# Where finished products leave PSUM, which engine does the differences, and the queue of the w_out jobs

## The chip, the cores and the metric

The kernel runs on one core of one Trainium2 chip. Its engines are TensorE (PE in the rows, PEld for its weight loads), VectorE (DVE), ScalarE (ACT), GpSimd (POOL) and SyncE (SP, here a queue that issues DMAs). Each works through its own instructions in order and waits for the others by semaphores. The metric is the device time of one execution in microseconds, the median of the runs of a kernel.

## The reference

A windowed attention over 4 x 576 tokens with 8 heads of 64, then two MLPs of width 512 and inner width 2048 over the 2304 tokens, all in float32:

```python
def reference(**kwargs):
    attn_out = _attn_ref(**attn_kwargs)
    x = attn_out.transpose(0, 2, 1, 3).reshape(B * S, H * D)
    x = _moe_ref(x=x, **moe_kwargs)
    return _moe2_ref(x=x, **moe2_kwargs)

def _moe_ref(x, w_in, w_out, s, b):
    h = x @ w_in
    r = np.maximum(h, 0.0)
    return (s * (r * r) + b) @ w_out

def _moe2_ref(x, w_in, w_out):
    h = x @ w_in
    return (h * np.cos(h)) @ w_out
```

## The kernel before

**Precision.** A float32 operand is cut into a high and a low part of TensorE's float32r form; a product is then three matmuls (high by high, high by low, low by high). A cut is a cast on ScalarE (the high part) and a difference on VectorE (the low part).

**First MLP.** 80 steps `p`: five token tiles of 384 or 512 columns (`t`), 16 blocks of the inner width each (`fc`). A step does `mm_in` (12 matmuls), `relu2` on ScalarE and VectorE, and `out_step` of the step two before (`LAG`; 12 matmuls). The attention and the work on the second MLP's weights are hung between the steps by `at(...)` and fired at three phases of a step.

**Jobs.** In the last 16 steps of the first MLP eight jobs prepare w_out of the second. `job_load(i)` fetches two raw blocks from DRAM into a tile `a` of seven slots, `job_sums(i)` fills the other slots (the seven weight combinations of a 2 by 2 product in seven multiplications), `job_split(i)` cuts them and stores both parts to `cut_out` in DRAM. Job 0 is summed in step 67, and the next ones follow at 1.5 steps on average. Tile `a` has two buffers, so the load of job i + 2 waits until the last store from job i's tile has landed. Loads and stores are issued by SP, in order with all its other DMAs.

**Second MLP.** Three token blocks `i` of 768 columns (`NS`), 16 inner blocks each: 48 steps `n`. Step `n` of the loop at the end issues `mm_h(n)`, 24 matmuls of 384 columns into a PSUM pair `h`, of which three are in turn, so that `mm_h(n)` needs `cos_g(n - 3)` to be done. The activation h cos h is a chain: `cos_n(n)` (ScalarE adds MAGIC), `cos_r(n)` (subtracts it again, on ScalarE or VectorE by its flag, then `r` on VectorE), `cos_q(n)` (VectorE), and a step later `cos_s(n - 1)` (two passes on ScalarE) and `cos_g(n - 1)` (VectorE, writes `G`).

The second product is done in seven products M1 to M7 over the 2 by 2 blocks of `G` and w_out. Each is four units `k` of 12 matmuls; `unit_cut(u)` cuts the operand of a unit, and `cut_to` runs it up to two units ahead of TensorE in the loop. Some operands are differences of others (`sub`). Units 0 to 3 run in steps 6, 10, 14 and 18, from step 19 on two in every step but 31 and 33, and the last 26 after the loop. So a product ends with every second step.

For the first two token blocks all products add up in one PSUM tile, `yy`:

```python
    fresh = j in ("M1", "M2", "M7") or (i == NS - 1 and j == "M4")
    ...
    if k == 3:
        evac[:] = [(i, j)]
```

After its last unit a product is in `evac`, and the next call of `evacuate()` copies it out: M1, M5 and M6 by `keep` on ScalarE (`s`, `v`, `r`), M3 by `send` on ScalarE, M2, M7 and M4 by `send` on VectorE (line 675, `o`). The next product's first unit waits for that copy. In the loop the call stands behind the chain of the step and ahead of its units; the units behind it are on TensorE after `mm_h(n)`.

Of the kernel before, what the change touches and what calls it, by code (L numbers as in the profile page):

```python
# [74 lines left out]
def attention_then_two_mlps(ctx, tc, qk_p, qk_d, v_p, v_d, mask_p, mask_d, w1, w2, sv, bv, out):  # L75
# [134 lines left out]
    def job_load(i):  # L210
        a = after_att[0].tile([P, 7, 256], F32, tag=f"job{i % 2}", name=f"job{i}")
        two = lambda fc: whole_out[fc].rearrange("p (e n) -> p e n", e=2)
        nc.sync.dma_start(a[:, 0:6:5, :], two(2 * i))
        nc.sync.dma_start(a[:, 4:7:2, :], two(2 * i + 1))
        jobs[i] = a

    def job_sums(i):
        a = jobs[i]
        for to, x, y, op in ((1, 5, 6, ALU.add), (2, 1, 0, ALU.subtract), (3, 4, 2, ALU.subtract), (5, 0, 5, ALU.subtract)):
            nc.gpsimd.tensor_tensor(out=a[:, to, :], in0=a[:, x, :], in1=a[:, y, :], op=op)  # L220

    def job_split(i):
        a = jobs.pop(i)
        for lo, hi in ((0, 4), (4, 7)):
            h = wpool.tile([P, hi - lo, 256], F32R, tag=f"wh{2 * (i % 2) + lo // 4}", name=f"jh{i}_{lo}")
            nc.scalar.copy(h, a[:, lo:hi, :])
            nc.vector.tensor_tensor(
                out=a[:, lo:hi, :].bitcast(F32R), in0=a[:, lo:hi, :], in1=h.bitcast(F32), op=ALU.subtract
            )
            nc.sync.dma_start(cut_out[:, lo:hi, i, 0, :], h.bitcast(F32))  # L230
        nc.sync.dma_start(cut_out[:, :, i, 1, :], a)
# [274 lines left out]
    def w_in_load(n):  # L506
        if n >= NH:
            return
        place, tag = (wpool, f"wl{n}") if n < 4 else (home[0], f"wi{n % 4}")
        win[n] = place.tile([P, 2, DM], F32R, tag=tag, name=f"wi{n}")  # L510
        nc.sync.dma_start(win[n].bitcast(F32), cut_in[n % NFC])
# [52 lines left out]
    def cos_g(n):  # L564
        i, fc = divmod(n, NFC)
        f, k, z = fc % 2, fc // 4, fc // 2 % 2
        if z == 0:
            G[i, f, k] = home[0].tile([P, 2, 2, SB], F32, tag=f"G{i % 2}{f}{k}", name=f"G{i}_{f}_{k}")
        g = G[i, f, k]
        nc.vector.scalar_tensor_tensor(  # L570
            out=g[:, :, z, :], in0=ns.pop(n), scalar=-1.0, in1=hp.pop(n), op0=ALU.add, op1=ALU.mult
        )
        if f == 0 and z == 1:
            sub(i, g[:, 1], g[:, 1], g[:, 0], nc.gpsimd)
            ops[i, k, "M1"], ops[i, k, "M5"] = g[:, 0], g[:, 1]
        if f == 1 and z == 1:
            ops[i, k, "M2"], ops[i, k, "M3"] = g[:, 0], g[:, 1]

    def sub(i, out, a, b, eng):
        eng.tensor_tensor(out=out, in0=a, in1=b, op=ALU.subtract)  # L580
# [12 lines left out]
    def unit_cut(u):  # L593
# [7 lines left out]
        if j == "M5" and not last:  # L601
            t2 = G[i, 0, k][:, 1]
            sub(i, t2, G[i, 1, k][:, 1], t2, nc.gpsimd)
            ops[i, k, "M6"] = t2
            b11 = G[i, 0, k][:, 0]
            sub(i, b11, t2, b11, nc.gpsimd)
            ops[i, k, "M7"] = b11
        if j == "M2" and last:
            t2 = home[0].tile([P, 2, SB], F32, tag=f"G{1 - i % 2}0{k}", name=f"t2_{k}")
            sub(i, t2, G[i, 1, k][:, 1], G[i, 0, k][:, 1], nc.gpsimd)  # L610
            ops[i, k, "M6"] = t2
            b11 = G[i, 0, k][:, 0]
# [65 lines left out]
    def evacuate():  # L678
# [4 lines left out]
        if i < NS - 1:  # L683
# [35 lines left out]
    with tc.manual_schedule():  # L719
# [216 lines left out]
        for n in range(1, NH):  # L936
# [17 lines left out]
            evacuate()  # L954
# [101 lines left out]
```

## Time and profile before

| what | value |
|---|---|
| median of 2 runs | 1008.63 us (1005.95 to 1011.32) |
| profiled execution, whole | 1007.53 us |
| its span, first to last instruction | 1005.70 us |
| mean granted clock of TensorE | 0.959 of full speed |
| TensorE busy | 910.3 us, 91% |
| VectorE busy | 638.4 us, 63% |
| ScalarE busy | 519.6 us, 52% |
| GpSimd busy | 142.2 us, 14% |

The span is that of the instructions; the execution's own time is 1.83 us longer. Busy time of TensorE is modelled from pipelined matmuls and hides stretches in which it runs at its lower clock, so the timeline in blocks of equal work says more than the share.

### The profile page before, as it was taken

To read this page: it belongs to the slowest core of one execution; us is meant where nothing else is said; L and a number is where in the kernel's file an instruction comes from. 1 tells how busy PE (TensorE), PEld (TensorE's weight loads), DVE (VectorE), ACT (ScalarE), POOL (GpSimd) and SP (SyncE) were. 2 spreads that over 40 slices of the span, in tenths; PEclk is the share of its full clock that TensorE was granted. 3 is DMA by queue.
4 is the path that set the end of the run, shared out by engine and by line. 5 is a ranking of instruction groups with operands and counts; after the bars stand their busy time and mean duration, and the time that the engine had idled before them with its cause. 6 is when DMAs were issued, how large, how long until landed. Compare 5 with 4: busy or idle time off the path is not lost. (4 is left out here: it accounts for less than half of the span.)

```text
span 1005.7 us, 13928 instructions
## 1 busy us (share of the span) xinstructions
PE 910.3 (91%) x5148; PEld 806.6 (80%) x5148; DVE 638.4 (63%) x1001; ACT 519.6 (52%) x1057; POOL 142.2 (14%) x94
## 2 busy tenths in 40 slices
PE   8999999999999999998788788878779888877888
PEld 6666699988888888886678788878779888877888
DVE  6888877665557665774436667655546655544753
ACT  6776777754556555544435655344334434333433
POOL 1000000000000000032220002502200430300740
PEclk9999999999999999999899999998889998999899
DMA  9956143343434554576798335444445454543566
GB/s 265 337 203 211 51 136 117 107 167 96 164 115 162 172 165 141 190 225 231 260 302 347 105 105 168 147 146 135 147 141 182 140 176 129 171 150 100 172 198 211
DMA packets 76050, 173.08 MB, mean 172 GB/s; under 512 B 7024, under 2 KB 35152, under 8 KB 75984
## 3 DMA queue, kind: packets, MB, share of 16 engines
q1 hardware_dynamic: 75840, 172.01, 52.4%
q8 instruction: 41, 0.67, 0.3%
q14 instruction: 25, 0.20, 0.1%
q10 hardware_dynamic: 144, 0.20, 0.1%
HBM read 135.48 MB, written 36.70 MB: 171 GB/s over the span
## 5 line engine op out<-in xcount | busy, mean ns | idle before, releaser
L645 PE MATMUL yy_M<-op,wo 128*128 128x384 f32 x1008 | 204.8, 364 | 59.6 <-DVE o L675 18.0
L645 PEld LDWEIGHTS yy_M<-op,wo 128*128 128x128 f32 x1008 | 196.1, 209 | 66.0 <-issue 29.2
L534 PE MATMUL h<-x,wi 128*128 128x384 f32 x1152 | 212.0, 341 | 19.4 <-issue 13.2
L534 PEld LDWEIGHTS h<-x,wi 128*128 128x128 f32 x1152 | 204.5, 192 | 22.9 <-issue 18.2
L543 ACT ACTIVATE n<-h,pmagic 128x768 f32<-128x768 f32 x48 | 43.1, 900 | 150.5 <-PE h L534 150.5
L599 DVE TENSOR_TENSOR op<-G,op 128x768 fp32r<-128x768 f32 x80 | 93.3, 1185 | 41.0 <-ACT op L598 41.0
L440 PE MATMUL y<-g,wh 128*128 128x512 f32 (+1 forms) x256 | 99.4, 388 | 8.6 <-DVE g L497 8.6
L598 ACT CAST op<-G 128x768 fp32r<-128x768 f32 x80 | 65.0, 830 | 77.1 <-PE yy_M L645 36.8
L425 PE MATMUL h<-xs,wh 128*128 128x512 f32 (+1 forms) x256 | 99.0, 387 | 0.0
L441 PE MATMUL y<-g,wh 128*128 128x512 f32 (+1 forms) x256 | 97.8, 382 | 0.2 <-DVE g L498 0.2
L442 PE MATMUL y<-g,wl 128*128 128x512 f32 (+1 forms) x256 | 97.6, 381 | 0.0
L427 PE MATMUL h<-xs,wl 128*128 128x512 f32 (+1 forms) x256 | 96.4, 377 | 0.0
L426 PE MATMUL h<-xs,wh 128*128 128x512 f32 (+1 forms) x256 | 96.4, 376 | 0.0
L550 DVE TENSOR_SCALAR n<-n 128x768 f32<-128x768 f32 x40 | 25.8, 644 | 109.1 <-ACT n L543 109.1
L220 POOL TENSOR_TENSOR job<-job 128x256 f32<-128x256 f32 x32 | 25.5, 808 | 477.8 <-DVE wa L145 407.9
L330 ACT ACTIVATE sm<-sm,nmax 96x80 f32<-96x80 f32 (+1 forms) x140 | 49.5, 355 | 49.2 <-DVE nmax L327 49.2
L580 POOL TENSOR_TENSOR G<-G 128x768 f32<-128x768 f32 x20 | 45.3, 2265 | 192.9 <-DVE G L570 169.3
L552 DVE SCALAR_TENSOR_TENSOR r<-n,h 128x768 f32<-128x768 f32 x48 | 45.8, 954 | 33.7 <-ACT n L548 26.7
L489 ACT ACTIVATE r<-h 128x512 f32<-128x512 f32 (+1 forms) x80 | 43.9, 548 | 43.2 <-PE h L427 39.4
L440 PEld LDWEIGHTS y<-g,wh 128*128 128x128 f32 x256 | 48.9, 191 | 16.8 <-DVE g L497 9.5
L497 DVE CAST g<-r 128x512 fp32r<-128x512 f32 (+1 forms) x64 | 26.6, 416 | 52.7 <-ACT r L495 47.0
L441 PEld LDWEIGHTS y<-g,wh 128*128 128x128 f32 x256 | 49.0, 191 | 8.4 <-DVE g L498 1.0
(104 smaller groups left out, 1423.0 us busy)
## 6 DMA issues: line engine op xcount, KB each, us to landing
wo<-cut_out SPq DMA_DIRECT2D x84, 512.0 KB, 4.1
wi<-cut_in SPq DMA_DIRECT2D x48, 512.0 KB, 5.1
stage<-w SPq DMA_DIRECT2D x32, 512.0 KB, 8.0
raw<-w SPq DMA_DIRECT2D x32, 512.0 KB, 4.9
cut_out<-job SPq DMA_DIRECT2D x8, 896.0 KB, 7.8
qk<-qk_d SPq DMA_DIRECT2D x20, 352.0 KB, 3.5
qk<-qk_p SPq DMA_DIRECT2D x20, 304.0 KB, 3.1
x<-y SPq DMA_DIRECT2D x12, 384.0 KB, 7.1
```

The costliest lines, as they stand in the source:

```text
L330: nc.scalar.activation(out=sm[:, j, :], in_=sm[:, j, :], func=AF.Exp, bias=nmax[:, j : j + 1], scale=1.0, accum_out=ssum[:, j : j + 1],)
L425: nc.tensor.matmul(h[:, : SIZES[t]], hi, x[:, 0, :], start=cc == 0, stop=False)
L426: nc.tensor.matmul(h[:, : SIZES[t]], hi, x[:, 1, :], start=False, stop=False)
L427: nc.tensor.matmul(h[:, : SIZES[t]], lo, x[:, 0, :], start=False, stop=cc == NCC - 1)
L440: nc.tensor.matmul(y[:, : SIZES[t]], hi, g[:, 0, :], start=fc == 0, stop=False)
L441: nc.tensor.matmul(y[:, : SIZES[t]], hi, g[:, 1, :], start=False, stop=False)
L442: nc.tensor.matmul(y[:, : SIZES[t]], lo, g[:, 0, :], start=False, stop=fc == NFC - 1)
L534: nc.tensor.matmul(h[:, t, :SB], wt, x[:, t * SB : (t + 1) * SB], start=cc == 0 and k == 0, stop=cc == NCC - 1 and k == 2,)
L552: nc.vector.scalar_tensor_tensor(out=r, in0=v, scalar=-C1, in1=hp[n], op0=ALU.mult, op1=ALU.add)
L598: nc.scalar.copy(x[:, 0], src)
L599: nc.vector.tensor_tensor(out=x[:, 1], in0=src, in1=x[:, 0].bitcast(F32), op=ALU.subtract)
L645: nc.tensor.matmul(b[:, eb, :SB], wt, g, start=fresh and k == 0 and z == 0 and n == 0, stop=k == 3 and z == 1 and n == 2, skip_group_check ...
```

## The change

- `evacuate()` is called at the head of a step, ahead of `cos_n(n)`, and no longer behind the step's chain.
- `cos_r(n)` stands ahead of `cos_s(n - 1)`; its first subtraction is on ScalarE for n above 17 (30 steps) and on VectorE up to 17, where before it was on ScalarE for the odd n below 17 (8 steps).
- All differences (`sub`, 52 of them) and the jobs' sums (32) go from GpSimd to VectorE.
- The low parts of a job get a tile of their own (`wl0` to `wl3`) in place of job tile `a`, and are stored in two DMAs per job. The jobs' loads and stores are issued by GpSimd. The first four w_in loads take `wl4` to `wl7`.

```diff
--- before.py
+++ after.py
@@ -210,25 +210,25 @@
     def job_load(i):
         a = after_att[0].tile([P, 7, 256], F32, tag=f"job{i % 2}", name=f"job{i}")
         two = lambda fc: whole_out[fc].rearrange("p (e n) -> p e n", e=2)
-        nc.sync.dma_start(a[:, 0:6:5, :], two(2 * i))
-        nc.sync.dma_start(a[:, 4:7:2, :], two(2 * i + 1))
+        nc.gpsimd.dma_start(a[:, 0:6:5, :], two(2 * i))
+        nc.gpsimd.dma_start(a[:, 4:7:2, :], two(2 * i + 1))
         jobs[i] = a
 
     def job_sums(i):
         a = jobs[i]
         for to, x, y, op in ((1, 5, 6, ALU.add), (2, 1, 0, ALU.subtract), (3, 4, 2, ALU.subtract), (5, 0, 5, ALU.subtract)):
-            nc.gpsimd.tensor_tensor(out=a[:, to, :], in0=a[:, x, :], in1=a[:, y, :], op=op)
+            nc.vector.tensor_tensor(out=a[:, to, :], in0=a[:, x, :], in1=a[:, y, :], op=op)
 
     def job_split(i):
         a = jobs.pop(i)
-        for lo, hi in ((0, 4), (4, 7)):
-            h = wpool.tile([P, hi - lo, 256], F32R, tag=f"wh{2 * (i % 2) + lo // 4}", name=f"jh{i}_{lo}")
+        for n, (lo, hi) in enumerate(((0, 4), (4, 7))):
+            h, l = (
+                wpool.tile([P, hi - lo, 256], F32R, tag=f"w{c}{2 * (i % 2) + n}", name=f"j{c}{i}_{n}") for c in "hl"
+            )
             nc.scalar.copy(h, a[:, lo:hi, :])
-            nc.vector.tensor_tensor(
-                out=a[:, lo:hi, :].bitcast(F32R), in0=a[:, lo:hi, :], in1=h.bitcast(F32), op=ALU.subtract
-            )
-            nc.sync.dma_start(cut_out[:, lo:hi, i, 0, :], h.bitcast(F32))
-        nc.sync.dma_start(cut_out[:, :, i, 1, :], a)
+            nc.vector.tensor_tensor(out=l, in0=a[:, lo:hi, :], in1=h.bitcast(F32), op=ALU.subtract)
+            nc.gpsimd.dma_start(cut_out[:, lo:hi, i, 0, :], h.bitcast(F32))
+            nc.gpsimd.dma_start(cut_out[:, lo:hi, i, 1, :], l.bitcast(F32))
 
 
     eppool = pool1("ep")
@@ -506,7 +506,7 @@
     def w_in_load(n):
         if n >= NH:
             return
-        place, tag = (wpool, f"wl{n}") if n < 4 else (home[0], f"wi{n % 4}")
+        place, tag = (wpool, f"wl{n + 4}") if n < 4 else (home[0], f"wi{n % 4}")
         win[n] = place.tile([P, 2, DM], F32R, tag=tag, name=f"wi{n}")
         nc.sync.dma_start(win[n].bitcast(F32), cut_in[n % NFC])
 
@@ -571,13 +571,13 @@
             out=g[:, :, z, :], in0=ns.pop(n), scalar=-1.0, in1=hp.pop(n), op0=ALU.add, op1=ALU.mult
         )
         if f == 0 and z == 1:
-            sub(i, g[:, 1], g[:, 1], g[:, 0], nc.gpsimd)
+            sub(g[:, 1], g[:, 1], g[:, 0])
             ops[i, k, "M1"], ops[i, k, "M5"] = g[:, 0], g[:, 1]
         if f == 1 and z == 1:
             ops[i, k, "M2"], ops[i, k, "M3"] = g[:, 0], g[:, 1]
 
-    def sub(i, out, a, b, eng):
-        eng.tensor_tensor(out=out, in0=a, in1=b, op=ALU.subtract)
+    def sub(out, a, b):
+        nc.vector.tensor_tensor(out=out, in0=a, in1=b, op=ALU.subtract)
 
 
     UNITS = [(i, j, k) for i in range(NS) for j in (PRODUCTS if i < NS - 1 else LAST) for k in range(4)]
@@ -600,21 +600,21 @@
         split[u] = x
         if j == "M5" and not last:
             t2 = G[i, 0, k][:, 1]
-            sub(i, t2, G[i, 1, k][:, 1], t2, nc.gpsimd)
+            sub(t2, G[i, 1, k][:, 1], t2)
             ops[i, k, "M6"] = t2
             b11 = G[i, 0, k][:, 0]
-            sub(i, b11, t2, b11, nc.gpsimd)
+            sub(b11, t2, b11)
             ops[i, k, "M7"] = b11
         if j == "M2" and last:
             t2 = home[0].tile([P, 2, SB], F32, tag=f"G{1 - i % 2}0{k}", name=f"t2_{k}")
-            sub(i, t2, G[i, 1, k][:, 1], G[i, 0, k][:, 1], nc.gpsimd)
+            sub(t2, G[i, 1, k][:, 1], G[i, 0, k][:, 1])
             ops[i, k, "M6"] = t2
             b11 = G[i, 0, k][:, 0]
-            sub(i, b11, t2, b11, nc.gpsimd)
+            sub(b11, t2, b11)
             ops[i, k, "M7"] = b11
         if j == "M2":
             b21 = G[i, 1, k][:, 0]
-            sub(i, b21, b21, ops[i, k, "M6"], nc.gpsimd)
+            sub(b21, b21, ops[i, k, "M6"])
             ops[i, k, "M4"] = b21
 
     yy = {}
@@ -686,7 +686,7 @@
                 keep(i, "s", b)
             elif j == "M5":
                 keep(i, "v", b)
-                sub(i, s["v"], s["v"], s["s"], nc.gpsimd)
+                sub(s["v"], s["v"], s["s"])
             elif j == "M6":
                 keep(i, "r", b)
             elif j == "M3":
@@ -695,7 +695,7 @@
                 send(i, 0, b, s["s"])
             elif j == "M7":
                 send(i, 3, b, s["r"])
-                sub(i, s["r"], s["r"], s["v"], nc.gpsimd)
+                sub(s["r"], s["r"], s["v"])
             else:
                 send(i, 2, b, s["r"])
             return
@@ -944,14 +944,14 @@
             if n in (3, 18):
                 for cc in range(NCC):
                     x_load(n // 16 + 1, cc)
+            evacuate()
             cos_n(n)
+            cos_r(n, n > 17)
             cos_s(n - 1)
-            cos_r(n, n < 17 and n % 2 == 1)
             cos_g(n - 1)
             cos_q(n)
             if n in x_at:
                 x_cut(*x_at[n])
-            evacuate()
             for _ in range(at_unit.get(n, 0)):
                 cut_to(nu + 1)
                 unit(nu)
```

VectorE where product M2 of token block 0 ends, from step 26 into step 27: `op20` and `op21` are cuts of step 26, `o0_0` is the copy that frees PSUM. Before:

```order
L557 SCALAR_TENSOR_TENSOR n2_26_6411<-n2_26_6411,r2_26_6416 128x768
L522 TENSOR_TENSOR x2_2_1_5832<-x2_2_1_5832,x2_2_0_5831 128x768
L599 TENSOR_TENSOR op20_6451<-G0_0_0_5169,op20_6451 128x768
L599 TENSOR_TENSOR op21_6454<-G0_0_1_5289,op21_6454 128x768
L550 TENSOR_SCALAR n2_27_6484<-n2_27_6484 128x768
L552 SCALAR_TENSOR_TENSOR r2_27_6489<-n2_27_6484,h2_27_6457 128x768
L570 SCALAR_TENSOR_TENSOR G1_0_2_6341<-n2_26_6411,h2_26_6384 128x2x384
L557 SCALAR_TENSOR_TENSOR n2_27_6484<-n2_27_6484,r2_27_6489 128x768
L675 SCALAR_TENSOR_TENSOR o0_0_6494<-yy0_M2_6347,s0_5903 128x768
L599 TENSOR_TENSOR op22_6526<-G0_0_2_5458,op22_6526 128x768
```

Now:

```order
L557 SCALAR_TENSOR_TENSOR n2_26_6435<-n2_26_6435,r2_26_6438 128x768
L522 TENSOR_TENSOR x2_2_1_5856<-x2_2_1_5856,x2_2_0_5855 128x768
L599 TENSOR_TENSOR op20_6475<-G0_0_0_5193,op20_6475 128x768
L599 TENSOR_TENSOR op21_6478<-G0_0_1_5313,op21_6478 128x768
L675 SCALAR_TENSOR_TENSOR o0_0_6508<-yy0_M2_6371,s0_5917 128x768
L552 SCALAR_TENSOR_TENSOR r2_27_6514<-n2_27_6511,h2_27_6481 128x768
L570 SCALAR_TENSOR_TENSOR G1_0_2_6368<-n2_26_6435,h2_26_6408 128x2x384
L580 TENSOR_TENSOR G1_0_2_6368<-G1_0_2_6368 128x768
L557 SCALAR_TENSOR_TENSOR n2_27_6511<-n2_27_6511,r2_27_6514 128x768
L599 TENSOR_TENSOR op22_6550<-G0_0_2_5482,op22_6550 128x768
```

The copy `o0_0` moved ahead of everything that needs `mm_h(27)`, the subtraction at L550 went to ScalarE, and a difference (L580) came in from GpSimd.

VectorE at the start of the tail, after `q` of step 47 (L557); `op60` to `op62` are cuts of M2's operands, `t2_0` and the lines L580 are differences. Before:

```order
L599 TENSOR_TENSOR op58_7912<-G2_0_2_7444,op58_7912 128x768
L599 TENSOR_TENSOR op59_7915<-G2_0_3_7735,op59_7915 128x768
L570 SCALAR_TENSOR_TENSOR G2_1_3_7808<-n2_47_7870,h2_47_7845 128x2x384
L599 TENSOR_TENSOR op60_7921<-G2_1_0_6932,op60_7921 128x768
L599 TENSOR_TENSOR op61_7942<-G2_1_1_7228,op61_7942 128x768
L599 TENSOR_TENSOR op62_7965<-G2_1_2_7521,op62_7965 128x768
```

Now:

```order
L599 TENSOR_TENSOR op58_7936<-G2_0_2_7471,op58_7936 128x768
L599 TENSOR_TENSOR op59_7939<-G2_0_3_7763,op59_7939 128x768
L570 SCALAR_TENSOR_TENSOR G2_1_3_7832<-n2_47_7897,h2_47_7869 128x2x384
L599 TENSOR_TENSOR op60_7945<-G2_1_0_6956,op60_7945 128x768
L580 TENSOR_TENSOR t2_0_7948<-G2_1_0_6956,G2_0_0_6919 128x768
L580 TENSOR_TENSOR G2_0_0_6919<-t2_0_7948,G2_0_0_6919 128x768
L580 TENSOR_TENSOR G2_1_0_6956<-G2_1_0_6956,t2_0_7948 128x768
L599 TENSOR_TENSOR op61_7966<-G2_1_1_7252,op61_7966 128x768
```

Three differences now stand between one M2 cut and the next.

The jobs' DMAs between the split of job 0 and the load of job 2, on SP before (with the DMAs of other work around them):

```order
L188 DMA raw30_4462<-w2 128x512
L230 DMA cut_out_123<-jh0_0_4489 128x4x256
L230 DMA cut_out_123<-jh0_4_4493 128x3x256
L231 DMA cut_out_123<-job0_4343 896x1x256
L213 DMA job2_4498<-whole_out4_111 128x2x256
L214 DMA job2_4498<-whole_out5_112 128x2x256
L205 DMA cut_in13_104<-raw29_4411 128x512
```

Now on GpSimd's queue:

```order
L214 DMA job1_4442<-whole_out3_110 128x2x256
L230 DMA cut_out_123<-jh0_0_4489 128x4x256
L231 DMA cut_out_123<-jl0_0_4490 128x4x256
L230 DMA cut_out_123<-jh0_1_4495 128x3x256
L231 DMA cut_out_123<-jl0_1_4496 128x3x256
L213 DMA job2_4501<-whole_out4_111 128x2x256
L214 DMA job2_4501<-whole_out5_112 128x2x256
```

A job has six DMAs there, one more than before, and nothing else is issued from that queue.

## Rows read from the trace of the kernel before

**Rows 1.** The page, parts 1 and 5: busy time; mean ns of one.

```profile
PE 910.3 (91%) x5148; PEld 806.6 (80%) x5148; DVE 638.4 (63%) x1001; ACT 519.6 (52%) x1057; POOL 142.2 (14%) x94
...
L599 DVE TENSOR_TENSOR op<-G,op 128x768 fp32r<-128x768 f32 x80 | 93.3, 1185 | 41.0 <-ACT op L598 41.0
...
L580 POOL TENSOR_TENSOR G<-G 128x768 f32<-128x768 f32 x20 | 45.3, 2265 | 192.9 <-DVE G L570 169.3
```

**Rows 2.** Timeline of TensorE, second MLP: start, length, matmuls, [idle time before].

```profile
628.43 4.32 PE L534 MATMUL h<-x,wi 128*128 128x384 f32 x24
...
702.46 5.97 PE L645 MATMUL yy_M<-op,wo 128*128 128x384 f32 x24 [3.30 <-ACT o L673]
...
726.48 5.93 PE L645 MATMUL yy_M<-op,wo 128*128 128x384 f32 x24 [5.55 <-DVE o L675]
...
764.39 8.48 PE L534 MATMUL h<-x,wi 128*128 128x384 f32 x48
...
786.82 4.33 PE L645 MATMUL yy_M<-op,wo 128*128 128x384 f32 x24
790.99 4.32 PE L534 MATMUL h<-x,wi 128*128 128x384 f32 x24
...
924.84 4.32 PE L534 MATMUL h<-x,wi 128*128 128x384 f32 x24
```

**Rows 3.** Stretches: length, busy time of each engine, granted clock, DMA share, GB/s.

```profile
720.00:740.00 20.00, 14.45 (x75) 14.15 (x74) 9.12 (x10) 7.39 (x10) 2.45 (x1) 0.83 0.40 130
```

**Rows 4.** Timeline of all engines, around the end of product M2.

```profile
720.96 0.90 ACT L543 ACTIVATE n<-h,pmagic 128x768 f32<-128x768 f32 x1 [3.62 <-PE h L534]
...
724.37 0.95 DVE L557 SCALAR_TENSOR_TENSOR n<-n,r 128x768 f32<-128x768 f32 x1
...
725.24 0.95 DVE L675 SCALAR_TENSOR_TENSOR o<-yy_M,s 128x768 f32<-128x768 f32 x1
```

**Rows 5.** Timelines of TensorE and of all engines, steps 4 to 11.

```profile
536.86 12.81 PE L534 MATMUL h<-x,wi 128*128 128x384 f32 x72 [1.72 <-DMA wi<-cut_in]
...
574.45 0.85 ACT L561 ACTIVATE n<-n 128x768 f32<-128x768 f32 x1 [2.11 <-DVE n L557]
...
576.08 0.92 ACT L548 ACTIVATE n<-n,nmagic 128x768 f32<-128x768 f32 x1
...
577.03 0.95 DVE L552 SCALAR_TENSOR_TENSOR r<-n,h 128x768 f32<-128x768 f32 x1 [2.62 <-ACT n L548]
...
580.51 0.55 DVE L550 TENSOR_SCALAR n<-n 128x768 f32<-128x768 f32 x1
```

**Rows 6.** Timelines of TensorE and of all engines, from step 47 to the end.

```profile
934.68 23.42 PE L645 MATMUL yy_M<-op,wo 128*128 128x384 f32 x121 [5.53 <-DVE o L675]
...
962.58 0.44 PE L645 MATMUL yy_M<-op,wo 128*128 128x384 f32 x1 [2.13 <-ACT op L598]
...
1001.84 0.49 ACT L667 ACTIVATE o<-yy_M 128x384 f32<-128x384 f32 x1 [5.41 <-PE yy_M L645]
```

**Rows 7.** The job stretch: timelines; SP's waits (total, times, longest); DMA issues (landing).

```profile
425.59 0.39 PE L440 MATMUL y<-g,wh 128*128 128x512 f32 x1
...
428.31 0.39 PE L425 MATMUL h<-xs,wh 128*128 128x512 f32 x1
...
447.55 0.53 SPq L213 DMA_DIRECT2D job<-whole_out  x1
...
485.74 0.80 PE L440 MATMUL y<-g,wh 128*128 128x512 f32 x1 [5.34 <-DVE g L497]
...
512.33 0.52 SPq L213 DMA_DIRECT2D job<-whole_out  x1
...
SPq L213 <- DMA cut_out<-job: 36.8, 6, 9.3
...
cut_out<-jh SPq DMA_DIRECT2D x8, 512.0 KB, 5.5
job<-whole_out SPq DMA_DIRECT2D x14, 256.0 KB, 3.3
```

## The prediction

> **What bounds the kernel now.** I read the page first: TensorE is busy 91% of the span [rows 1], so the question is where the other 9%, and its slow stretches, lie. The second view is TensorE's timeline over the second MLP [rows 2]. A block of 24 matmuls (one `mm_h`, or two units) takes 4.17 us when nothing waits (786.82 to 790.99). Steps 19 to 30 have 24 blocks and should take 100.1 us; they take 135.96 (628.43 to 764.39). Steps 35 to 46 take 133.85 (790.99 to 924.84). So 35.9 + 33.8 = 69.7 us are lost there, in twelve waits. Each stands ahead of the first unit of a new product: the units add into one PSUM tile, the next product may not touch it until the finished one has been copied out, and the copy is queued behind `cos_n(n)`, which waits for this step's `mm_h`. A copy by ScalarE costs 3.30 us of idle time and a block of 5.97 instead of 4.33 behind it, one by VectorE 5.55 us and 5.93 [rows 2]; the granted clock from 720 to 740 is 0.83, a mix of its levels of 1.2 and 2.4 GHz [rows 3].
>
> The same reckoning elsewhere. Step 31 to 34: 26.60 us for six blocks, 1.6 lost [rows 2]. Steps 4 to 18: 91.57 us (536.86 to 628.43) for 15 `mm_h` and four units of 2.085, 20.7 lost [rows 2, 5]. The tail: `mm_h(47)` ends at 929.0, the last matmul at 1001.84; 28 units are 58.4 us, 14.4 lost [rows 2, 6]. The stretch of the w_out jobs: 425.59 to 536.86 holds 27 blocks of 2.72 (425.59 to 428.31) and four `mm_h`, 90.1 us, 21.2 lost [rows 5, 7].
>
> **Products leave PSUM at the head of the step.** The copy is now ahead of `cos_n(n)` on its engine; it can run while TensorE does `mm_h(n)`, 4.17 us. On ScalarE nothing stands between it and the last unit, so those waits (s, v, r and the negated M3) go. On VectorE the copy `o` queues behind the cuts of the step before. From the start of `cos_n` (720.96) count 0.90, the subtraction of MAGIC 0.92 and two sine passes of 0.85 on ScalarE, together 3.5; then `G`, `q`, perhaps an x cut, two operand cuts and `o` on VectorE at a spacing of 0.87 and a last length of 0.95 [rows 4, 5]. `o` ends at 8.0, with an x cut at 8.85; TensorE arrives at about 8.15. Two boundaries (steps 27 and 29) keep 0.7 us each. I leave 1.7 for all: **68 us** gained, and 1.4 of step 31 to 34's 1.6. The block behind a wait that is gone runs at 4.17, as the others do.
>
> **All sums on VectorE.** 52 differences leave POOL. There one takes 2.3 us and holds VectorE up: a cut `op` takes 1.19 on average [rows 1], against 0.95 for operations of its size [rows 4]. On VectorE they cost 52 x 0.87 = 45 us; it gets back 80 x 0.24 = 19 us from the cuts alone, and 22 passes of some 0.66 (30 now on ScalarE, 8 before): 14 us. Net about +12 us over 480, so the engine is not the bound as a whole. Locally: a step that cuts two M5 operands has ten VectorE operations and runs about 2.2 us past its 8.34; the cut its units need is the fifth and eighth of them, due a step later, so I charge nothing.
>
> **The first half of the stage.** On odd steps the sine passes (574.45), then the subtraction of MAGIC (576.08) on ScalarE, then `r` (577.03), `G` and `q` on VectorE make one loop of 1.63 + 0.95 + 3 x 0.87 + 0.1 = 5.3 us from one `q` to the next [rows 5]; TensorE needs 4.17, or 4.69 with its share of a unit. With the subtraction on VectorE (0.55 [rows 5], some 0.66 with the gap to the next) `r` is done during the sine passes, and the loop is 1.7 + 0.95 + 0.95 = 3.6. VectorE then has 16.6 us of work in four steps (13.1 for them, 3.5 for two x cuts, one operand cut and one difference) against TensorE's 18.8. Where the last three fall into one step (7, 11, 15) the next `G` is late by some 1.4 us. Stepping through leaves 6.5 of the 20.7: **14 us** gained.
>
> **The tail.** No `mm_h` follows step 47, so the two units that hid the cuts of 58 and 59 are followed by them at once. Counted from 929.0: `G(46)` starts at 3.6, then a difference, `q`, and the cut of 58 ends at 7.1; the units end at 4.2, so TensorE waits 3.0. Each M2 operand then costs VectorE a cut and three differences, 3.5 us, against 2.085 of TensorE; with what is in hand that makes three more waits of 1.4. Sum 7.2 instead of 14.4, of which 5.5 is now the product boundary at 934.68 and 2.1 one wait for an operand [rows 6]: **7 us** gained.
>
> **The jobs' tiles and queue.** Today a job's load waits on SP for the store of the job two before it: 36.8 us in six waits, and the loads follow each other every 13.0 us (447.55 to 512.33, five spacings) where the program's steps would have 1.5 x 5.44 = 8.2 [rows 7]. ScalarE's `jh` copy stands behind the late load, `relu2` behind that, and TensorE idles 5.34 us at 485.74 [rows 7]. The new low tile frees the job tile at once, and SP's weight loads no longer queue behind jobs. Against this stand four sums of 256 columns per job on VectorE (a third to the whole of 0.95 each, 1.3 to 3.8 us; I take the third), which now block `g` in order if a load is late, and six DMAs per job on POOL's queue, of which the trace has none. If they cost what SP's do, 0.53 to issue and 3.3 to 5.5 to land [rows 7], a job keeps to 8.2 us and up to 19 us come back. If each must land before the next starts, a job takes 2 x 3.3 + 4 x 5.5 = 28.6. A job now takes 13.0; the wait that goes is 6.1 of it. I take 10.6, halfway from 8.2 to 13.0: six jobs slip 14 us, **7 us** gained of 21.2. The first four w_in loads move to the tiles wl4 to wl7, last read at steps 70 to 73 and loaded at 75 to 78: free of cost, and the bytes moved stay the same.
>
> VectorE's cuts stretch beside POOL's sums [rows 1], so POOL's issues may stretch beside VectorE.
> The Trainium skill (SBUF — State Buffer, section "SBUF: two separate sides") speaks against this part: descriptors of a DMA issued from POOL are written by POOL, which is locked out while VectorE runs a one-input pass at double rate, and it gives 3100 ns where 620 would do. By its factor of five an issue of 0.53 would be an estimated 2.6 us, a job 15.9, and this part would lose 25 us instead of gaining 7. No run here shows it. The skill (DMA: Bandwidth & Descriptors, section "Issuing engines are not separate DMA queues") adds that another issuing queue saves only the issuer's time. The 36.8 us above are of that kind, in order on SP, so by that rule the 7 us stand.
>
> **The sum.** 68 + 1.4 + 14 + 7 + 7 = 97.4 us. The profiled execution took 1007.53, 1.1 under the median of 1008.63; 1007.53 - 97.4 = **910 us**.
>
> **Rivals.**
> (a) POOL's queue is behind VectorE. With 16 us per job (2.6 per issue, between SP's 0.53 and a landing) six jobs slip 6 x 7.8 = 47, less 21.2 now: 26 lost instead of 7 gained, 943 us. For it: VectorE is loaded in the stretch, and `g` waits in order. Against: two job tiles let loads run ahead.
> (b) VectorE's new work gets in the way. Eight steps with M5 or M2 cuts have 1.7 to 3.5 us more; if that falls on TensorE (8 x 2.6 = 21) and half of the gain in steps 4 to 18 goes with it (7), 938 us. Against it: the count above, and 19 us returned.
> (c) **Slower.** POOL moves one DMA at a time, each landed before the next: 28.6 us a job, 6 x 20.4 - 21.2 = 101 lost against 90.4 gained elsewhere, 1018 us. It decides from 27 us a job on, 4.5 us per DMA. For it: landings of 3.3 and 5.5. Against it: nothing but that it is the far end of the bounds.
> (d) The change does not do what it says: the copy is issued early, but its engine has not finished the cuts, and half of each wait stays: 1007.53 - 97.4 + 34 = 944.
>
> **Chances.** My forecast (886 to 925) 0.62, (a) 0.15, (b) 0.10, (c) 0.04, (d) 0.04, better than 886 0.05. Low bound: waits all gone (69.7 + 1.6), 17, 11 and 19 give 889, a little under it for what the clock returns: 886. High bound: (a), (b) and (d) lie at 938 to 944; with a smaller 62 at the boundaries and 10 elsewhere, 17 lost at the jobs, 952. Faster by over 2% (about what a measurement of this kernel can tell from no change, 20 us) takes in all but (c) and worse forms of (d): 0.94; within 2% 0.04, where (c) stands; slower 0.02, for a job of over 30 us.
>
> **What would show it.** TensorE's timeline from step 19 to 46 in blocks of 4.2 us without "<-ACT" or "<-DVE o"; waits of 1 to 2 us left in steps 8, 12 and 16 and four waits in the tail; VectorE's cuts at 0.95; POOL with nothing but DMA issues, and the jobs' loads 8 to 13 us apart. It is wrong if TensorE waits at `g` in the job stretch for more than 21 us, or if units wait for `op` in steps 34 to 41.

## The result, and the profile after

The changed kernel takes 935.62 us (median of two, 935.20 and 936.05) where the kernel before takes 1008.63: a ratio of 0.928 [0.917 to 0.938]. The range of 886 to 952 holds it; the forecast's own band of 886 to 925, around 910, does not; 935.6 lies in the part that was set by rivals. The profiled execution took 935.2 with a span of 933.4, so 72.3 us less than the 1007.53 that the sum was made against.

I cut both timelines of TensorE at the same four points: the start of an `out_step` at 425.59 (the two traces agree up to there), the start of `mm_h(4)`, of `mm_h(19)`, the end of `mm_h(47)`, and the last matmul. Before, the four stages are 111.3, 91.6, 300.6 and 72.8 us [rows 2, 5 to 7]. After, they are 119.2, 87.0, 230.7 and 67.1. (Where a group of matmuls runs through a cut I count blocks of 4.16 from its start: `mm_h(1)` to `mm_h(4)` start at 532.26, so `mm_h(4)` at 544.7.)

The boundaries first. TensorE's timeline after, from step 27 to the end: start, length, matmuls, [idle time before].

```profile
703.23 4.40 PE L645 MATMUL yy_M<-op,wo 128*128 128x384 f32 x24 [0.64 <-issue]
...
720.75 4.40 PE L645 MATMUL yy_M<-op,wo 128*128 128x384 f32 x24 [0.64 <-issue]
724.99 4.32 PE L534 MATMUL h<-x,wi 128*128 128x384 f32 x24
...
733.31 8.48 PE L534 MATMUL h<-x,wi 128*128 128x384 f32 x48
...
858.20 4.32 PE L534 MATMUL h<-x,wi 128*128 128x384 f32 x24
862.36 4.90 PE L645 MATMUL yy_M<-op,wo 128*128 128x384 f32 x25
869.82 12.31 PE L645 MATMUL yy_M<-op,wo 128*128 128x384 f32 x60 [2.56 <-DVE op L599]
883.36 2.38 PE L645 MATMUL yy_M<-op,wo 128*128 128x384 f32 x12 [1.23 <-DVE op L599]
886.95 16.77 PE L645 MATMUL yy_M<-op,wo 128*128 128x384 f32 x95 [1.22 <-DVE op L599]
904.25 25.20 PE L645 MATMUL yy_M<-op,wo 128*128 128x384 f32 x144 [0.53 <-DMA wo<-cut_out]
```

Twelve waits of 3.3 or some 5.5 us [rows 2] are down to two of 0.64, at the two steps that the prediction names. In the tail four waits are left, 5.5 us in all: three for an operand and one for a load of weights.

The page after, parts 1 and 5: GpSimd has nothing but the 48 DMA issues of the jobs and ten short operations in the first 18 us, and VectorE's cut is back at 0.952 us, where [rows 1] had 1185 ns.

```profile
PE 888.3 (95%) x5148; PEld 788.6 (84%) x5148; DVE 646.7 (69%) x1063; ACT 540.9 (58%) x1079; POOL 39.7 (4%) x58
...
L599 DVE TENSOR_TENSOR op<-G,op 128x768 fp32r<-128x768 f32 x80 | 74.4, 952 | 14.5 <-ACT op L598 14.5
```

Steps 4 to 18, and the job stretch ahead of them, on TensorE's timeline after.

```profile
476.37 0.79 PE L440 MATMUL y<-g,wh 128*128 128x512 f32 x1 [7.10 <-DVE g L497]
...
489.30 0.79 PE L440 MATMUL y<-g,wh 128*128 128x512 f32 x1 [5.02 <-DVE g L497]
...
513.93 0.80 PE L440 MATMUL y<-g,wh 128*128 128x512 f32 x1 [5.49 <-DVE g L497]
...
532.26 12.91 PE L534 MATMUL h<-x,wi 128*128 128x384 f32 x73
...
554.52 10.82 PE L534 MATMUL h<-x,wi 128*128 128x384 f32 x48 [5.33 <-issue]
...
567.28 12.64 PE L534 MATMUL h<-x,wi 128*128 128x384 f32 x72
...
581.23 4.39 PE L534 MATMUL h<-x,wi 128*128 128x384 f32 x24 [1.31 <-issue]
...
601.50 4.43 PE L534 MATMUL h<-x,wi 128*128 128x384 f32 x24 [1.31 <-issue]
...
623.79 6.00 PE L534 MATMUL h<-x,wi 128*128 128x384 f32 x24 [3.29 <-issue]
...
631.71 4.32 PE L534 MATMUL h<-x,wi 128*128 128x384 f32 x24
```

Here is the miss. TensorE waits for `g` more than before, and the two steps from 554.52 start 5.33 us late and take 10.82 where two blocks take 8.48. The waits show who is late; totals, times and longest, in us, from 425 to 560, after:

```profile
DVE job L220 <- DMA job<-whole_out: 41.8, 6, 14.7
...
POOL cut_out L231 <- issue: 29.8, 7, 7.2
...
ACT n L543 <- DMA cut_out<-jh: 7.6, 1, 7.6
```

VectorE now waits for the jobs' loads, in order, with `g` behind it, and the loads are late because GpSimd issues them late. The last line belongs to the two late steps: `cos_n` on ScalarE waits there for the landing of a late store of the jobs, and `mm_h(5)` waits for what follows from that `cos_n`. One round of jobs on GpSimd's queue after (start, length of the issue, [idle time before]):

```profile
485.84 0.77 POOL L230 DMA_DIRECT2D cut_out<-jh  x1 [2.18 <-issue]
489.54 0.77 POOL L231 DMA_DIRECT2D cut_out<-jl  x1 [2.93 <-DVE g L497]
490.30 0.75 POOL L230 DMA_DIRECT2D cut_out<-jh  x1
493.26 0.76 POOL L231 DMA_DIRECT2D cut_out<-jl  x1 [2.21 <-DVE g L497]
494.55 0.74 POOL L213 DMA_DIRECT2D job<-whole_out  x1 [0.53 <-issue]
495.29 0.73 POOL L214 DMA_DIRECT2D job<-whole_out  x1
498.19 0.77 POOL L230 DMA_DIRECT2D cut_out<-jh  x1 [2.17 <-issue]
```

An issue takes 0.73 to 0.77 us, so GpSimd is not slow at it. But it stands still ahead of four of these seven, for 2.2 to 2.9 us, and mostly for nothing that the profile shows; pauses of this length or longer come at the same places in most rounds, so the `g` named in two rows is only the last event. The distances fit landings: 3.70 from the first `jh` to its `jl` and 3.72 from there to the second `jl`, where the jobs' DMAs on this queue land 3.0 to 4.5 us after issue (medians by kind). It looks as if one or two DMAs fill the queue and the next has to wait until they have landed. The job takes 12.35 us by that (485.84 to 498.19), and from job 2 to job 7 the loads are 14.4 us apart (448.84 to 520.82, five spacings).

### The profile page after: what moved, and what is told of

It reads as the page before. It is cut to its first block, busy times and chain, and to the rows that moved or that the text cites. A ratio compares the mean times of both kernels' runs of the same rounds, so it can differ in the third digit from the quotient of the medians.

```text
span 933.4 us, 13908 instructions
## 1 busy us (share of the span) xinstructions
PE 888.3 (95%) x5148; PEld 788.6 (84%) x5148; DVE 646.7 (69%) x1063; ACT 540.9 (58%) x1079; POOL 39.7 (4%) x58
## 4 chain that ended last, share of the span: by engine, by line
PE 77%; DVE 8%; issue 6%; DMA 5%; ACT 2%; POOL 1%; SPq 1%; DVEq 0%; POOLq 0%
PE h L534 21%; PE yy_M L645 16%; PE h L425 5%; PE h L427 4%; PE h L426 4%; PE y L440 4%; PE y L441 4%; PE y L442 4%; PE y L437 4%; PE h L419 3%; PE sc L300 3%; DMA job<-whole_out 2%; PE pv L376 2%; PE tp L351 1%; DVE jl L229 1%
## 5 line engine op out<-in xcount | busy, mean ns | idle before, releaser
L534 PE MATMUL h<-x,wi 128*128 128x384 f32 x1152 | 209.8, 339 | 11.2 <-issue 11.2
L645 PE MATMUL yy_M<-op,wo 128*128 128x384 f32 x1008 | 183.1, 337 | 6.9 <-DVE op L599 5.0
L645 PEld LDWEIGHTS yy_M<-op,wo 128*128 128x128 f32 x1008 | 176.4, 189 | 9.3 <-DVE op L599 5.9
L440 PE MATMUL y<-g,wh 128*128 128x512 f32 (+1 forms) x256 | 101.5, 396 | 18.9 <-DVE g L497 18.9
L441 PE MATMUL y<-g,wh 128*128 128x512 f32 (+1 forms) x256 | 99.6, 389 | 0.2 <-DVE g L498 0.2
L599 DVE TENSOR_TENSOR op<-G,op 128x768 fp32r<-128x768 f32 x80 | 74.4, 952 | 14.5 <-ACT op L598 14.5
L440 PEld LDWEIGHTS y<-g,wh 128*128 128x128 f32 x256 | 50.1, 196 | 28.2 <-DVE g L497 20.6
L570 DVE SCALAR_TENSOR_TENSOR G<-n,h 128x768 f32<-128x768 f32 x48 | 45.7, 953 | 19.5 <-ACT n L562 19.4
L441 PEld LDWEIGHTS y<-g,wh 128*128 128x128 f32 x256 | 49.9, 195 | 9.6 <-DVE g L498 1.9
L442 PEld LDWEIGHTS y<-g,wl 128*128 128x128 f32 x256 | 49.9, 195 | 8.0
L425 PEld LDWEIGHTS h<-xs,wh 128*128 128x128 f32 x256 | 48.1, 188 | 7.8
```

What stands on the lines that cost most here:

```text
L425: nc.tensor.matmul(h[:, : SIZES[t]], hi, x[:, 0, :], start=cc == 0, stop=False)
L440: nc.tensor.matmul(y[:, : SIZES[t]], hi, g[:, 0, :], start=fc == 0, stop=False)
L441: nc.tensor.matmul(y[:, : SIZES[t]], hi, g[:, 1, :], start=False, stop=False)
L442: nc.tensor.matmul(y[:, : SIZES[t]], lo, g[:, 0, :], start=False, stop=fc == NFC - 1)
L534: nc.tensor.matmul(h[:, t, :SB], wt, x[:, t * SB : (t + 1) * SB], start=cc == 0 and k == 0, stop=cc == NCC - 1 and k == 2,)
L599: nc.vector.tensor_tensor(out=x[:, 1], in0=src, in1=x[:, 0].bitcast(F32), op=ALU.subtract)
```

## The experiments

Theory A: the jobs' DMAs wait for room in GpSimd's queue, and everything else of the change does what was forecast. Rival B: GpSimd writes its DMAs slowly because VectorE is in its way. Rival C: the sums on VectorE hold `g` up in order, on whatever queue the DMAs are. Runs without an interval are one execution each; the kernel before took 1006.49 us beside e1 to e4, 1005.97 beside e5 to e9, and 1006.99 beside e10 and e11 (medians of 7, 7 and 6).

The stages by kernel, cut as above, in us (425.59 for all; in the other traces the same matmul starts up to 0.8 us from it):

| kernel | 425.59 to mm_h(4) | to mm_h(19) | to end of mm_h(47) | to last matmul | time |
|---|---|---|---|---|---|
| before | 111.3 | 91.6 | 300.6 | 72.8 | 1008.6 |
| after | 119.2 | 87.0 | 230.7 | 67.1 | 935.6 |
| e1_ring | 98.6 | 80.7 | 230.7 | 66.6 | 906.7 |
| e2_sp | 92.9 | 79.5 | 230.7 | 66.4 | 901.0 |
| e3_sumpool | 217.1 for both | | 230.7 | 66.3 | 946.6 |
| e4_head | 109.3 | 94.7 | 233.3 | 71.4 | 940.0 |
| e5_subpool | 93.3 | 79.5 | 233.6 | 71.7 | 909.5 |
| e6_cos | 92.8 | 90.2 | 228.9 | 65.6 | 909.1 |
| e8_lazy | 93.7 | 75.9 | 259.7 | 69.4 | 930.2 |
| e9_low | 97.8 | 80.6 | 230.7 | 66.3 | 907.4 |
| e10_spread | 93.5 | 78.5 | 230.7 | 63.4 | 896.9 |
| e11_ring96 | 100.4 | 80.5 | 230.7 | 66.3 | 909.3 |

The edit of e4_head touches neither of the first two stages, and they differ from those of the kernel before by 2.0 and 3.1 us. Differences of that size in these two columns are not read as effects.

**e1_ring: more room in GpSimd's queue.**

```
-    nc = bacc.Bacc("TRN2", target_bir_lowering=False, num_devices=1, dynamic_dma_scratch_size=1024)
+    nc = bacc.Bacc("TRN2", target_bir_lowering=False, num_devices=1, dynamic_dma_scratch_size=2048)
```

> The changed kernel with dynamic_dma_scratch_size 2048 in place of 1024, nothing else; the jobs' DMAs stay on GpSimd's queue. Theory A (the queue holds only one or two of these DMAs at a time, so GpSimd waits 2.2 to 2.9 us between two issues for room, five times per job, and a job takes 12.3 us): with twice the room these waits go or halve, the loads of jobs 3 to 7 follow each other every 8 to 10 us, the stretch from 425.59 to mm_h(4) falls from 128.9 to some 100 to 110 us, and the time is 910 to 920 us. Theory B (GpSimd writes its DMAs slowly because VectorE is in its way) and theory C (the sums on VectorE hold g up in order, whatever the queue): no change, 933 to 938 us, loads still 12 to 14 us apart.

Measured: 906.68 us, ratio 0.902 [0.899 to 0.904]. One number in the program's head, no instruction changed, and 29 us are back; that is 3 us better than the range. GpSimd's queue in e1_ring, the same part of a round:

```profile
485.11 0.77 POOL L231 DMA_DIRECT2D cut_out<-jl  x1 [0.72 <-DVE g L498]
486.32 0.73 POOL L213 DMA_DIRECT2D job<-whole_out  x1 [0.44 <-issue]
487.05 0.86 POOL L214 DMA_DIRECT2D job<-whole_out  x1
487.90 0.78 POOL L230 DMA_DIRECT2D cut_out<-jh  x1
490.02 0.76 POOL L231 DMA_DIRECT2D cut_out<-jl  x1 [1.35 <-DVE jl L229]
490.77 0.75 POOL L230 DMA_DIRECT2D cut_out<-jh  x1
491.97 0.76 POOL L231 DMA_DIRECT2D cut_out<-jl  x1 [0.44 <-issue]
493.24 0.73 POOL L213 DMA_DIRECT2D job<-whole_out  x1 [0.51 <-issue]
```

The pauses of 2.2 and 2.9 are gone from these rows; now the queue waits for the data (`jl`), 1.35. The loads come 6.92 us apart here and 10.0 on average (job 2 at 443.07 to job 7 at 493.24, five spacings), since twice, near 467 and 480, they still stand 3.3 and 1.7 us. Theory A holds; B and C, which expected no change, fall. The one wait of TensorE for `g` that is left is 4.92 us. From 470 to 500 the DMA engines move 351 GB/s in e1_ring, on the same queue.

**e11_ring96: half of that room.** The same line with 1536.

> The changed kernel with dynamic_dma_scratch_size 1536, halfway between its 1024 and the 2048 of e1_ring. Theory A (the queue's room sets how long a job takes): between the two, 911 to 928 us, GpSimd's waits between issues shorter than 2.2 to 2.9 us but still there. If 2048 helped for another reason than room (a place in memory, a threshold that 2048 passes): 933 us or more, as with 1024, or 907 as with 2048.

Measured: 909.34 us, between my two cases (911 to 928, and 907 as with 2048): 26 of the 29 us are had with the first 512. The executions of e1_ring lie from 904.6 to 908.0, so the times alone hardly tell 1536 from 2048. The pauses do: GpSimd's waits for a `jl` issue that nothing visible ended fall from 29.8 us to 14.7 and, with 2048, to 6.6. That they fall step by step fits a queue whose room grows; it leaves little of the rival that 2048 passes some threshold.

**e2_sp: the jobs' DMAs on SP's queue.**

```
-        nc.gpsimd.dma_start(a[:, 0:6:5, :], two(2 * i))
+        nc.sync.dma_start(a[:, 0:6:5, :], two(2 * i))
...
-            nc.gpsimd.dma_start(cut_out[:, lo:hi, i, 0, :], h.bitcast(F32))
-            nc.gpsimd.dma_start(cut_out[:, lo:hi, i, 1, :], l.bitcast(F32))
+            nc.sync.dma_start(cut_out[:, lo:hi, i, 0, :], h.bitcast(F32))
+            nc.sync.dma_start(cut_out[:, lo:hi, i, 1, :], l.bitcast(F32))
```

(The second load likewise.)

> The changed kernel with the jobs' six DMAs back on SP's queue; the low tiles, the sums on VectorE and all else stay. Theory A (GpSimd's queue is the miss): the stretch from 425.59 to mm_h(4) falls below the kernel before's 111.3, to 98 to 111 us, since the wait of a load for the store of the job two before is gone, and the time is 904 to 918 us. Theory C (the sums on VectorE hold g up): the stretch stays at 125 or more and the time is above 930 us.

Measured: 900.96 us, ratio 0.897 [0.894 to 0.901]; a little better than expected. It is 5.7 us under e1_ring, for the most part by the job stretch (92.9 against 98.6), where e1_ring still has pauses. The jobs' loads on SP in e2_sp:

```profile
475.14 1.36 SPq L213 DMA_DIRECT2D job<-whole_out  x1
...
482.89 1.11 SPq L213 DMA_DIRECT2D job<-whole_out  x1
...
490.67 1.01 SPq L213 DMA_DIRECT2D job<-whole_out  x1
```

They are 7.8 us apart here, 8.2 from job 3 to job 7 (457.70 to 490.67, four spacings): the program's schedule of 8.2, which the prediction had as its lower end. TensorE's waits in the stretch shrink to under 1 us each. Busy times of PE, PEld, DVE, ACT, POOL, then granted clock, DMA share and GB/s, from 470 to 500, first after and then e2_sp:

```profile
470.00:500.00 30.00, 18.61 (x60) 14.11 (x61) 13.16 (x23) 9.12 (x13) 9.78 (x13) 0.77 0.55 189
```

```profile
470.00:500.00 30.00, 29.31 (x133) 24.33 (x132) 21.91 (x38) 16.01 (x24) 0.00 (x0) 1.00 1.05 362
```

It is the same span of time, not the same work. After, the DMA engines move 189 GB/s, and TensorE's granted clock is 0.77 on average, a mix of its levels of 1.2 and 2.4 GHz, with waits of 7.10 and 5.02 us in this span (at 476.37 and 489.30) and slow matmuls behind them; in e2_sp they move 362 and the clock stays at 1.00.

**e3_sumpool: the jobs' sums back on GpSimd, with their DMAs.** In `job_sums`, `nc.vector` becomes `nc.gpsimd`.

> The changed kernel with the 4 x 8 sums of the jobs back on GpSimd, whose queue also has the jobs' DMAs; all else stays. Theory A: sums and DMAs now stand in one order on GpSimd, each job's sums wait there for its load, so a job takes 12.3 us plus some 3 to 6, and the time is 945 to 970 us. Theory C (sums on VectorE hold g up): VectorE waits less, the stretch falls to some 110 us and the time is 915 to 922 us.

Measured: 946.60 us. 11 us worse than after, as A has it: on GpSimd the sums stand in one row with the pauses. C is refuted a second time.

**e9_low: sums on GpSimd, DMAs on SP.** Both edits, so only the low tile is new for the jobs.

> The kernel of e2_sp with the jobs' sums back on GpSimd, so that of the change to the jobs only the low tile is left (the DMAs are on SP there). If the low tile, which ends the wait of a load for the store of the job two before, is what shortens the job: the stretch to mm_h(4) is 93 to 98 us, where e2_sp has 92.9, and the time is 900 to 907 us. If the sums on VectorE carry it (0.42 us each in place of 0.81): the stretch goes back to 105 or more and the time is over 912 us.

Measured: 907.35 us, 0.4 over the upper end. The stretch is 97.8: of the 18.4 us between before (111.3) and e2_sp (92.9) the low tile brings 13.5 and the sums on VectorE 4.9, taken in this order, with one execution of e9_low.

**e4_head: the kernel before, with `evacuate()` ahead of `cos_n(n)` alone.**

```
+            evacuate()
             cos_n(n)
             cos_s(n - 1)
...
-            evacuate()
```

> The kernel before with one edit: the copies out of PSUM (evacuate) stand at the head of a step, ahead of cos_n, and no longer at its end. Theory A for the boundaries (the place of the copy alone makes the twelve waits): steps 19 to 30 and 35 to 46 fall from 136.0 and 133.9 us to 100 to 106 each, and the time is 940 to 950 us. The rival (the differences on GpSimd stretch VectorE's cuts, so a copy on VectorE is late even at the head): the waits of two or three us at the boundaries whose copy is on VectorE stay, the two parts take 110 to 120 each, and the time is 960 to 980 us.

Measured: 940.02 us, 66 under the kernel before. Steps 19 to 47 take 233.3 us where they took 300.6. So 67.3 of the 69.9 us are the place of the copy alone; the differences on GpSimd still cost there (cuts of 1281 ns, and these waits for an operand, which after does not have in these steps):

```profile
L599 DVE TENSOR_TENSOR op<-G,op 128x768 fp32r<-128x768 f32 x80 | 100.1, 1281 | 14.5 <-ACT op L598 14.4
```

```profile
769.44 4.28 PE L645 MATMUL yy_M<-op,wo 128*128 128x384 f32 x23 [0.41 <-DVE op L599]
...
779.27 2.36 PE L645 MATMUL yy_M<-op,wo 128*128 128x384 f32 x12 [1.22 <-DVE op L599]
```

**e5_subpool: e2_sp with the 52 differences on GpSimd.** In `sub`, `nc.vector` becomes `nc.gpsimd`.

> The kernel of e2_sp with the 52 differences (sub) back on GpSimd, all else as there. If the differences stretch VectorE's cuts (1.28 us each beside them, 0.95 without) and that reaches TensorE: steps 4 to 18 are 2 to 6 us longer than the 79.5 of e2_sp, steps 19 to 47 some 2.7 longer (as the kernel before with the copies at the head showed), the tail 4 to 5 longer than 66.4, and the time is 908 to 916 us. If their place does not matter once the copies stand at the head: 899 to 904 us.

Measured: 909.45 us. Steps 4 to 18 do not move (79.5), where I had expected 2 to 6 more; steps 19 to 47 lose 2.9, the tail 5.3. The differences on VectorE are worth some 8 us, none of it in the first half.

**e6_cos: e2_sp with the cosine in the old order.**

```
-            cos_r(n, n > 17)
             cos_s(n - 1)
+            cos_r(n, n < 17 and n % 2 == 1)
```

> The kernel of e2_sp with the cosine in the order of the kernel before: cos_s ahead of cos_r, and the subtraction of MAGIC on ScalarE on odd steps up to 16, on VectorE on all others. By the prediction's loop of 5.3 us on odd steps, steps 4 to 18 take 88 to 92 us in place of 79.5 and the time is 909 to 914 us. By the rival (the differences on GpSimd were what held steps 4 to 18 up, the cosine's order is free): 899 to 904 us, and e5_subpool shows the loss instead.

Measured: 909.05 us. Steps 4 to 18 are 90.2, and the waits of the kernel before are back, two in every four steps; steps 9 and 10 on TensorE's timeline of e6_cos:

```profile
547.69 4.43 PE L534 MATMUL h<-x,wi 128*128 128x384 f32 x24 [1.15 <-issue]
...
553.68 4.43 PE L534 MATMUL h<-x,wi 128*128 128x384 f32 x24 [1.56 <-issue]
```

So 10.7 of the 12.1 us of the first half (91.6 to 79.5) are the edit of the cosine, its order and its flag together. Behind step 18 the old form is the better one: steps 19 to 47 take 228.9 us where e2_sp takes 230.7, without a wait at steps 27 and 29, and the tail 65.6 in place of 66.4. Old behind step 18 and new up to it was not run.

**e8_lazy: each difference right ahead of the cut that needs it.** The tuples that `unit_cut` put into `ops` hold a difference still to be made, and this makes it:

```
-        src = ops[i, k, j]
+        src = operand(i, k, j)
...
+    def operand(i, k, j):
+        if isinstance(ops[i, k, j], tuple):
+            out, a, b = ops[i, k, j]
+            a, b, out = a(), b(), out()
+            sub(out, a, b)
+            ops[i, k, j] = out
+        return ops[i, k, j]
```

> The kernel of e2_sp with each difference put right ahead of the cut that needs it, in place of two or three of them behind one cut; the same 36 differences of operands on VectorE in another order. By the prediction's reading of the waits that are left (a cut and three differences, 3.5 us, per M2 unit in the tail; two cuts and three differences ahead of the next G at steps 14 and 18): the two waits of 1.2 in the tail go and the one of 2.6 shrinks, the 3.3 of step 18 goes to 1.5 or less, and the time is 890 to 897 us. By the rival (these waits are due to the number of VectorE's operations in a stretch, not to their order): 899 to 903 us.

Measured: 930.18 us, ratio 0.924 [0.921 to 0.926]. A miss of 33 us. The part that I had looked at came: step 18's wait falls from 3.29 to 1.30 and steps 4 to 18 from 79.5 to 75.9. But waits at the boundaries are back, and steps 19 to 47 take 29 us more; in the tail eight waits of 0.40 to 0.55 stand in place of two of 1.24, and it takes 69.4 where e2_sp takes 66.4. VectorE's timeline of e8_lazy in the step in which M2 leaves PSUM:

```profile
666.72 0.95 DVE L580 TENSOR_TENSOR G<-G 128x768 f32<-128x768 f32 x1
668.57 0.96 DVE L599 TENSOR_TENSOR op<-G,op 128x768 fp32r<-128x768 f32 x1 [0.90 <-ACT op L598]
669.45 0.95 DVE L580 TENSOR_TENSOR G<-G 128x768 f32<-128x768 f32 x1
671.35 0.96 DVE L599 TENSOR_TENSOR op<-G,op 128x768 fp32r<-128x768 f32 x1 [0.95 <-ACT op L598]
672.23 0.95 DVE L680 SCALAR_TENSOR_TENSOR o<-yy_M,s 128x768 f32<-128x768 f32 x1
```

A cut is a copy on ScalarE and a subtraction on VectorE. With the difference right ahead, ScalarE waits for it, and VectorE waits for ScalarE: 2.78 us from one cut to the next of which 0.95 is idle, and the copy `o` comes at 672.23 where e2_sp has it at 668.48. The copy `v` on ScalarE stands behind a waiting ScalarE in the same way, and TensorE waits 2.33 us for it at 618.50.

**e10_spread: one difference behind each cut.** M7's goes from the cut of M5 (M2 in the last slice) to that of M6; M4's in the last slice from M2 to M7.

```
+        if j == "M6":
             b11 = G[i, 0, k][:, 0]
-            sub(b11, t2, b11)
+            sub(b11, ops[i, k, "M6"], b11)
             ops[i, k, "M7"] = b11
...
-        if j == "M2":
+        if j == ("M7" if last else "M2"):
```

> The kernel of e2_sp with the 36 differences of operands spread so that each cut that has any is followed by one: M6's behind the cut of M5 (of M2 in the last slice), M7's behind the cut of M6, M4's behind the cut of M2 (of M7 in the last slice). None stands ahead of the cut that needs it, as in e8_lazy, and none comes in twos or threes. If the waits left in e2_sp come from the bunches: the two waits of 1.24 in the tail go, the 3.29 of step 18 falls to 1.3 to 1.5 with a faster block behind it, the boundaries stay at 0.64, and the time is 893 to 897 us. If e8_lazy lost its time to the spreading itself (a difference in a step in which a product leaves PSUM): boundaries of 2 us and more come back and the time is 905 to 930 us.

Measured: 896.86 us, ratio 0.890 [0.886 to 0.893], the best of all kernels here. TensorE's timeline of e10_spread, step 18 and the tail:

```profile
589.70 5.96 PE L534 MATMUL h<-x,wi 128*128 128x384 f32 x24 [2.29 <-issue]
...
835.77 55.98 PE L640 MATMUL yy_M<-op,wo 128*128 128x384 f32 x311 [2.55 <-DVE op L599]
```

The two waits of 1.24 in the tail are gone and the boundaries stay; step 18 gives 1.0 instead of the 1.8 to 2.0 expected, and the block behind it is as slow as before. So in the tail the bunches of differences were the waits, at step 18 only in part; 2.29 us stay there without a cause shown. And e8_lazy lost its time to the order of difference and cut, not to spreading as such.

## Why the prediction was right, and where a term was wrong

**Boundaries and steps 31 to 34: right.** Forecast 68 + 1.4, measured 69.9 (300.6 to 230.7), with 0.64 left where 0.7 was forecast. e4_head shows that the copy's place is 67.3 of it, so the reason holds and not only the sum. I had charged VectorE's new work nothing; that is right there, and e5_subpool shows that leaving the differences on GpSimd would have cost 2.9.

**The first half: right in its mechanism, 1.7 too much, which is within the scatter of this stage.** Forecast 14. After loses 16.1 of 87.0, but 7.7 of that is the late start and slow run of the two steps at 554.52, which belongs to the jobs (`cos_n` waits 7.6 us for a store of the jobs; in e1_ring and e2_sp, with the jobs on time, the late start does not occur). Without it the stage is 79.3: 12.3 gained. The edit of the cosine brought it (e6_cos), as the loop of 5.3 us has it. The three waits come from VectorE's full steps 7, 11 and 15, as I wrote, but on TensorE they stand ahead of `mm_h` of steps 10, 14 and 18, not in 8, 12 and 16. Two are 1.31; the third is 3.29 with a slow block behind it, where I had counted 1.4: two cuts and two differences stand ahead of the cosine that it needs.

**The tail: 5.8 instead of 7.** The first wait and two of the three behind it came, 2.56, 1.23 and 1.22 against 3.0 and 1.4 each; the fourth, 0.53, is for a load of weights, not for an operand. The waits are 5.5 in place of 7.2, and still the stage is longer than forecast: its blocks take 3.2 us more than the 58.4 that I had counted at full speed (from 869.8 to 882.1 the granted clock is 0.86). The gain was also put down to the wrong edit: I ascribed 5.5 to the copy's place; e4_head gains 1.4 by it, and e5_subpool shows 5.3 for the differences on VectorE.

**The jobs: wrong.** Forecast 7 gained; measured 15.6 lost (7.9 up to `mm_h(4)` and 7.7 behind it). This is 22.6 of the 25.1 us by which the profiled execution (935.2) misses 910.1; the rest is 1.7 and 1.2 of the two terms above, less 0.5 at the boundaries. The step that failed is the price of GpSimd's queue: "I take 10.6, halfway from 8.2 to 13.0". A job takes 12.35 at best and 14.4 on average. The rule from price to loss held: six jobs of 14.4 lose 6 x 6.2 - 21.2 = 16.0 us, and 15.6 was measured. Neither end of my bounds was the mechanism: an issue is nearly as cheap as SP's before (0.73 to 0.78 against 0.53), and the DMAs land in 3.0 to 4.5 us, where SP's took 3.3 to 5.5 [rows 7]. What I left out between "as SP" and "one at a time" is that the queue runs out of room after one or two of these DMAs, as the spacing of the issues and the three sizes have it, and that a number in the program's head, which the prediction does not mention, sets how much there is. Rival (c), one landing after another, was the right kind with too large a price, and I gave it 0.04; rival (a) came near the time (943) by a price of 2.6 us per issue that no row shows. So it was partly luck that the range held the time: its upper end rests on rivals (a), (b) and (d), none of whose mechanisms occurred, and on 17 us lost at the jobs without a mechanism of their own.

The rest of that part held: e9_low gives 13.5 to the low tile, and e2_sp shows that with the queue out of the way the stretch keeps to the schedule of 8.2, 2.8 us over the ideal 90.1. The sums on VectorE, which I had counted as a cost, brought 4.9. With the jobs' DMAs left on SP the change would have been worth 18.4 there instead of 7.

The Trainium skill (SBUF — State Buffer, section "SBUF: two separate sides") gives 3100 ns in place of 620 for a whole DMA issued from GpSimd beside certain copies on VectorE, and I had put that factor on the issue. Every issue of a job here took 0.72 to 0.97 us, in e1_ring as in after, so a loss came, but for another reason.

The Trainium skill (DMA: Bandwidth & Descriptors, section "Issuing engines are not separate DMA queues") says that DMAs initiated on several engines save only the time that it takes to initiate them. The 36.8 us that I set beside this rule are waits for stores, not time to initiate, so it did not speak for the 7 us. Here GpSimd's queue with 1024 cost 34.7 us against SP's (935.6 and 901.0): moving a DMA can also lose, and more than an issue's time.

Rivals (b) and (d) did not occur: no unit waits for `op` from step 19 to step 47, and of the boundaries' waits 1.3 us are left, not half.

My own test failed too. I had written that TensorE's waits at `g` of more than 21 us would show this part wrong; they add up to 18.9. The loss was also in slow-clock blocks behind the waits and in the two steps at 554.52, which no wait for `g` counts. The sign that did show it is the other one, loads 8 to 13 us apart.

## What to carry to other kernels

Moving DMAs to another queue needs that queue's depth as well as its price per issue: look for issues that follow each other at about a landing's distance with no releaser, and give the queue room, or use the queue that has it. In this kernel copies out of an accumulator belonged ahead of the step's own dependent work, but that place is only as early as the work queued before it: a cut that goes back and forth between two engines delays it again. When several short operations are owed behind one cut, spread them one behind each cut (e10_spread, 896.9 us); right ahead of the cuts they made the engines wait for each other (e8_lazy, 930.2).

## What the runs showed of the hardware

- DMAs issued from GpSimd can stand in line without a reason that the profile names: with `dynamic_dma_scratch_size` 1024 GpSimd stands for 2.1 us or more ahead of half of the issues (256 to 512 KB each), and 189 GB/s is moved from 470 to 500; the kernel takes 935.6 us with 1024, 909.3 with 1536 and 906.7 with 2048, and 901.0 with the same DMAs on SP. In the same span of time 351 GB/s is moved with 2048 and 362 with the DMAs on SP. That it is the room for descriptors which runs out fits the three sizes; no row shows the room itself.
- An issue of a job's DMA from GpSimd took 0.72 to 0.97 us in after, e1_ring, e3_sumpool and e11_ring96; VectorE was busy for 13 of the 30 us from 470 to 500 in after and for 20 in e1_ring.
- A 128x768 subtraction on VectorE takes 0.95 us, and 1.28 on average where GpSimd's differences run beside it (e4_head and e5_subpool).
